# Loading x of batch 1 in front of the states, with every step of a hand-ordered attention and PReLU kernel placed anew

## The chip, the cores and the metric

The kernel runs on one core of one Trainium2 chip. The metric is the device time of one execution in microseconds, lower is better. The profiler takes one further execution of the same program; its span runs from the first to the last instruction, and its own time is given beside the median of the timed runs.

## The reference, cut to what matters

x is (8 batches, 8 heads, 512 tokens, 64), state is (8, 8, 32, 64), the model width 512 = 8 heads x 64, the hidden width 2048. Everything is float32 outside.

```python
def _attn_ref(x, state):
    scores = scale * np.matmul(x, state.transpose(0, 1, 3, 2))     # tokens read the states
    a = softmax(scores)
    xread = np.matmul(a, state)
    scores2 = scale * np.matmul(state, x.transpose(0, 1, 3, 2))    # states read the tokens
    a2 = softmax(scores2)
    sread = np.matmul(a2, x)
    return np.concatenate([xread, sread], axis=2)

def _moe_ref(x, w_in, w_out, alpha):
    h = x @ w_in
    g = np.maximum(h, 0.0) + alpha * np.minimum(h, 0.0)
    return g @ w_out
```

The output of the attention, 8 x (512 + 32) rows of 512, is the input of the second function.

## The kernel before

**What is computed where.** The token half of the attention never forms `xread`: state times w_in is made once per batch (`m`, four pieces f of 512 hidden columns, from quarter f of w_in), and the hidden layer of a batch is softmax weights times `m` (`F`, one of 16 pieces of 128 hidden rows by 512 tokens, two matmuls of 512 columns). `N` on ACT makes the negative part, `G` on DVE the PReLU result g. For batch 0 the output product is direct (`S`, sums over hidden pieces into one bank per 128 tokens, then `O` out); batches 1 to 7, and the state rows of all batches taken as batch 8, use a seven-product scheme of Strassen's kind (`P`, four matmuls of 256 columns each, into the banks px, py and pv). Its sums of weights are `W` and its sums of g are `U`, both on POOL; `K` saves an intermediate px, `Q` makes a quarter of the output and sends it with one or two DMAs on SP's queue.

**The softmax of a batch.** x of batch b is loaded as float16 by a casting DMA of 512 KB on POOL's queue (`lx.b`), transposed by a DMA on SP's queue (`xd.b`; for batches 0 and 1 by PE, `xt`, with copies `xo`), and multiplied with the states (`sc.b`). From `sc` two chains start: for the tokens' weights `sb`, `smax`, `ssh`, `sexp`, `ssum`, `snorm`, `wb` and then the first `F` of the batch; for the states' own reading `tm`, `nb`, `te`, `tsum`, `tn`, `tt` (a DMA transpose), `rd`. Batch 0 uses its own path (`tsc`, `smax`, `ssh`, `sexp`, `ssum`, `snorm`, then `at` on PE and the copies `ao`).

**The opening.** Half of x of batch 0 comes by two plain DMAs on SP's and ACT's queues (`dx`, then the casts `cx`), the other half by a casting DMA on POOL's queue (`dxp.1`, 256 KB). The states of batch 0 come on SP's queue (`dst`; `stc` casts, `stt` transposes, `sto` and `sbd` copy), those of batches 1 to 7 in two casting DMAs of 112 KB on POOL's queue (`lst.0`, `lst.1`; `str` transposes a half of them on PE, `sro` copies it). The quarters of w_in (`wi`) and w_out (`wo`), 512 KB each, follow on POOL's queue. `Z.k.n` are filler matmuls of n x 128 columns on a constant tile, in bank k, that compute nothing which is used.

**What sets the order.** The whole program is one string of steps, `ORDER` (lines 19 to 99). A loop at the end of the kernel (the dictionary `steps`) calls one small function for each token, in that order, so each engine's queue holds its instructions in the order of the string. The numbers and letters of a token are its arguments: batch and piece, the PSUM bank (the last number of `F`, `f`, `xt`, `str`, `rd` and of the first `P` of a bank; the last two of some `m`), and the engine (`a` ACT, `v` DVE, `p` POOL, `s` SP). Six banks, 0 to 5, are given out by these numbers; two more form one tile named `two`, which `sc` and the `m` without bank numbers use in turn. A bank can be written again only when the last reader of its former content is done.

**Lines.** `lx` is L162, `dxp` L172, `dx` L182, `lst` L223, `wi` L232, `wo` L238, `Z` L261, `str` L274, `xt` L325, `xo` L330, `sc` L340, `at` L391, `snorm` L439, `rd` L509, `m` L536, `mo` L560 and L562, `F` L589, `f` (a half of two `F` of batch 0) L611, `N` L642, `G` L645, `S` L659, `W` L703, `U` L727, `P` L748, `K` L764, `Q` L779 to L787.

```python
    for token in (globals().get("TOKENS") or ORDER).split():
        name, *args = token.split(".")
        steps[name](*[int(a) if a.isdigit() else a for a in args])
```

Of the kernel before, what the change touches and what calls it, by code (L numbers as in the profile page):

```python
# [29 lines left out]
tsum.1 S.0.0.0 sc.0.0 sc.0.1 m.0.3.1.3 mo.0.3.a.1 mo.0.3.a.0 tm.0 S.0.1.1.4 S.0.1.0 nb.0.a S.0.1.2 F.0.14.1 te.0.1  # L30
S.0.1.3 ssum.1.3 snorm.v.1 tn.1.1.p tn.1.0.p N.0.14 F.0.15.0 S.0.0.4 S.0.1.4 te.0.0 m.1.3 N.0.15 mo.1.3.a S.0.1.5
tsum.0 F.0.12.3 W.2.0.p tn.0.1.p N.0.12 G.0.15 tn.0.0.p S.0.3.4 F.0.13.0 G.0.14 N.0.13 wb.1 G.0.12 tt.0 m.1.2 S.0.1.7
F.1.7.1 N.1.7 xd.2 W.3.0.p F.1.2.3 N.1.2 G.0.13 S.0.0.6 G.1.7 W.2.1.p F.1.6.0 S.0.1.6 G.1.2 F.1.12.1 N.1.6 O.0.1.v
tt.1 S.0.0.5 F.1.3.3 G.1.6 F.1.5.4 S.0.0.7 W.4.1.p mo.1.2.a F.1.15.0 S.0.3.5 N.1.12 G.1.12 F.1.14.1 N.1.3 N.1.5 N.1.15
G.1.3 O.0.0.a W.3.1.p N.1.14 S.0.3.6 S.0.3.7 W.4.0.p G.1.5 G.1.15 G.1.14 m.2.2.3.4 sc.2 mo.2.2.a.0 rd.0.0 mo.2.2.a.1
F.1.1.1 F.1.4.4 rdo.0.a O.0.3.a F.1.8.0 sb.2 N.1.1 S.0.2.2.5 tm.2 smax.2 N.1.8 lx.3 F.1.13.2 N.1.4 G.1.4 nb.2.a
S.0.2.7 S.0.2.0 ssh.p.2 S.0.2.6 S.0.2.4 te.2.1 F.1.0.4 rd.1.3 G.1.1 te.2.0 G.1.8 N.1.13 m.3.2 m.2.3.0.1 N.1.0 tsum.2
G.1.13 rdo.1.v sexp.2 S.0.2.1 S.0.2.5 S.0.2.3 G.1.0 mo.2.3.a.1 F.1.11.4 mo.3.2.a F.1.9.1 P.1.1.1.1.3 P.1.1.0.0
mo.2.3.a.0 ssum.2.2 lx.4 O.0.2.a N.1.11 F.1.10.0 N.1.10 U.1.1.1.p snorm.v.2 P.1.1.1.0 str.1.5 wb.2 m.2.1 N.1.9 sro.1.a
P.1.1.0.1 F.2.15.2 G.1.11 N.2.15 G.1.10 P.1.2.1.1.4 tn.2.0.p P.1.2.0.1 G.1.9 mo.2.1.a F.2.1.5 F.2.14.1 N.2.1 P.1.2.0.0  # L40
m.3.1 G.2.15 m.3.0.0.2 xd.3 K.1.1.v G.2.1 P.1.2.1.0 U.1.3.1.p F.2.0.5 N.2.14 mo.3.0.a.0 mo.3.0.v.1 F.2.11.0 tn.2.1.p
mo.3.1.a G.2.14 tt.2 N.2.0 U.1.2.1.p U.1.1.0.p Q.1.0.0 F.2.2.2 N.2.11 P.1.6.0.1 G.2.0 U.1.2.0.p m.5.0 N.2.2 U.1.3.0.p
G.2.11 U.1.4.1.p rd.2.4 P.1.6.1.1 m.4.0.1.5 rdo.2.v mo.5.0.a m.3.3.4.0 sc.3 G.2.2 P.1.6.1.0 sb.3 mo.4.0.a.0 mo.3.3.a.0
mo.3.3.a.1 tm.3 F.2.7.1 F.2.5.2 P.1.7.1.1.4 P.1.6.0.0 mo.4.0.a.1 N.2.7 F.2.4.0 F.2.13.5 G.2.7 N.2.5 P.1.7.0.1 K.1.2.a
nb.3.a P.1.5.0.0 G.2.5 N.2.4 N.2.13 U.1.4.0.p P.1.5.1.0 smax.3 F.2.9.2 P.1.7.0.0 te.3.1 lx.5 F.2.8.1 G.2.13 te.3.0
P.1.5.0.1 G.2.4 N.2.9 N.2.8 G.2.9 F.2.3.5 tsum.3 P.1.5.1.1 xd.4 ssh.p.3 N.2.3 F.2.10.0 K.1.4.a F.2.12.2 G.2.8 N.2.10
P.1.7.1.0 G.2.3 N.2.12 F.2.6.1 P.1.3.1.1 G.2.10 G.2.12 m.6.0 sexp.3 m.4.1.0.5 P.1.3.1.0 P.1.3.0.1 N.2.6 Q.1.1.1
mo.4.1.a.1 mo.6.0.a mo.4.1.a.0 tn.3.0.p G.2.6 tn.3.1.p ssum.3.2 P.1.3.0.0 U.2.1.0.p P.1.4.0.1 m.6.1.1.5 m.4.3
mo.6.1.a.0 P.1.4.1.1 P.1.4.1.0 P.1.4.0.0 mo.6.1.a.1 P.2.1.1.1.1 snorm.v.3 P.2.1.1.0 mo.4.3.a Q.1.0.1.v wb.3 m.4.2.2.5
m.5.3.0.3 sc.4 mo.4.2.a.1 P.2.1.0.0 mo.5.3.a.1 U.2.1.1.p F.3.15.5 mo.4.2.a.0 Q.1.1.0 P.2.1.0.1 U.2.2.1.p F.3.4.3  # L50
mo.5.3.a.0 F.3.12.4 F.3.1.2 K.2.1.a F.3.8.0 N.3.15 sb.4 tm.4 U.2.2.0.p N.3.12 N.3.4 P.2.6.0.1 N.3.1 nb.4.a G.3.15
G.3.12 P.2.6.0.0 N.3.8 F.3.6.5 N.3.6 P.2.6.1.0 xd.5 G.3.4 G.3.1 G.3.6 P.2.6.1.1 G.3.8 U.2.3.0.p F.3.3.4 F.3.7.3
K.2.2.a te.4.1 N.3.3 F.3.14.2 smax.4 U.2.4.1.p P.2.5.1.0 N.3.14 tt.3 U.2.4.0.p G.3.14 F.3.2.0 N.3.2 ssh.p.4 P.2.5.1.1
P.2.5.0.0 te.4.0 F.3.11.5 P.2.5.0.1 G.3.3 N.3.7 G.3.2 F.3.0.2 rd.3.4 K.2.4.a sc.5 P.2.3.1.0 N.3.0 U.2.3.1.p P.2.3.0.1
G.3.7 N.3.11 G.3.0 rdo.3.a F.3.10.3 tm.5 P.2.7.1.0.0 tsum.4 P.2.3.1.1 G.3.11 P.2.3.0.0 N.3.10 tn.4.0.p nb.5.a F.3.9.4
sexp.4 P.2.7.0.0 P.2.7.0.1 Q.2.0.1.a G.3.10 P.2.7.1.1 P.2.2.0.0.2 lx.6 ssum.4.3 N.3.9 P.2.2.1.0 G.3.9 P.2.2.1.1
F.3.13.1 te.5.1 te.5.0 U.3.1.0.p Q.2.1.1 tn.4.1.a P.2.2.0.1 tsum.5 P.2.4.0.0 N.3.13 snorm.v.4 P.2.4.1.1 F.3.5.4
P.2.4.1.0 P.2.4.0.1 Q.2.0.0 wb.4 P.3.1.0.0.3 F.4.5.5 N.3.5 U.3.2.0.p tt.4 P.3.1.1.0 tn.5.0.a N.4.5 tn.5.1.p G.3.5
F.4.3.2 F.4.8.4 G.3.13 N.4.3 U.3.1.1.p Q.2.1.0 N.4.8 F.4.2.1 P.3.1.1.1 N.4.2 G.4.5 F.4.7.0 P.3.1.0.1 U.3.2.1.p G.4.3
F.4.14.2 U.3.3.1.p N.4.7 K.3.1.a G.4.8 tt.5 F.4.9.5 N.4.14 U.3.4.0.p G.4.2 G.4.7 F.4.10.4 U.3.3.0.p F.4.12.1 P.3.6.0.0  # L60
N.4.9 U.3.4.1.p G.4.14 P.3.6.1.0 F.4.11.0 N.4.12 P.3.6.0.1 G.4.9 N.4.10 F.4.6.5 P.3.6.1.1 sb.5 rd.4.2 lx.7 N.4.11
G.4.11 N.4.6 K.3.2.a G.4.12 xd.6 G.4.10 rdo.4.a rd.5.0 m.6.3 m.7.0.2.1 F.4.13.4 P.3.5.1.1 rdo.5.a P.3.5.0.0 mo.6.3.a
G.4.6 N.4.13 mo.7.0.v.0 F.4.15.2 m.7.3.5.0 sc.6 mo.7.0.a.1 smax.5 F.4.4.1 P.3.5.0.1 G.4.13 P.3.5.1.0 mo.7.3.a.0
P.3.7.1.1.5 N.4.15 mo.7.3.a.1 F.4.0.4 N.4.4 F.4.1.0 P.3.7.0.0 K.3.4.a P.3.7.0.1 sb.6 G.4.15 N.4.0 P.3.2.0.0.2 tm.6
P.3.7.1.0 P.3.3.1.1 P.3.3.0.0 smax.6 P.3.2.1.0 N.4.1 G.4.1 P.3.2.0.1 nb.6.a ssh.p.5 Q.3.1.1 te.6.0 P.3.2.1.1 P.3.4.0.0
G.4.0 P.3.4.1.1 sexp.5 te.6.1 G.4.4 Q.3.0.0 ssh.p.6 ssum.5.4 P.3.4.1.0 sexp.6 snorm.v.5 P.3.3.0.1 P.4.2.0.1.1 m.5.2
U.4.1.1.p m.6.2.0.2 U.4.1.0.p wb.5 P.3.4.0.1 P.4.2.1.1 mo.6.2.a.0 P.3.3.1.0 mo.6.2.a.1 mo.5.2.a xd.7 Q.3.0.1.a
U.4.2.1.p P.4.1.1.0.0 P.4.1.0.1 P.4.1.1.1 m.7.2.2.4 m.5.1 Q.3.1.0 mo.7.2.a.0 F.5.12.3 P.4.2.1.0 ssum.6.5 P.4.1.0.0
tsum.6 mo.7.2.a.1 mo.5.1.a K.4.1.a F.5.0.2 snorm.v.6 N.5.12 P.4.2.0.0 F.5.2.4 Q.4.0.0 U.4.2.0.p P.4.6.1.1 F.5.15.5
F.5.8.1 sc.7 P.4.6.0.1 P.4.6.1.0 G.5.12 N.5.2 P.4.6.0.0 G.5.2 tn.6.0.p N.5.0 G.5.0 N.5.15 U.4.3.0.p F.5.9.4 N.5.8  # L70
K.4.2.a G.5.15 F.5.1.3 N.5.1 F.5.5.2 G.5.8 tm.7 F.5.3.1 F.5.10.5 G.5.1 P.4.5.0.0 P.4.5.0.1 N.5.5 N.5.3 N.5.9 N.5.10
nb.7.a G.5.5 G.5.3 F.5.11.3 P.4.5.1.1 G.5.10 tn.6.1.p N.5.11 te.7.1 P.4.5.1.0 U.4.4.0.p F.5.6.2 K.4.4.a G.5.9
U.4.3.1.p U.4.4.1.p G.5.11 F.5.14.5 F.5.4.1 F.5.7.4 N.5.6 P.4.7.1.0.3 sb.7 P.4.7.1.1 P.4.3.1.0 P.4.3.0.0 N.5.14 N.5.7
P.4.7.0.1 P.4.7.0.0 G.5.6 P.4.3.1.1 F.5.13.2 P.4.3.0.1 te.7.0 G.5.7 G.5.14 N.5.13 U.5.1.0.p tt.6 wb.6 tsum.7 F.6.13.5
# [764 lines left out]
```

## Time and profile before

| what | value |
|---|---|
| median of 3 runs | 209.1 us (208.94 to 209.68) |
| the profiled execution's own time | 210.77 us |
| its span | 208.6 us |
| granted TensorE clock, mean | 0.997 |
| busy: PE | 202.1 us (97%) |
| busy: DVE | 174.8 us (84%) |
| busy: POOL | 181.5 us (87%) |
| busy: ACT | 146.1 us (70%) |

The profile's page gives busy time by engine, slices of the span, the chain of work that ended last, and groups of equal instructions. PE's share needs care: a matmul's end is modelled and overlaps the start of the next, so the distance from one start to the next is the true price. A row of the timeline gives the start, the length and the number of merged instructions; the bracket at its end is the idle time of the engine just before, and what ended it.

### The profile page before, as it was taken

Reading aid. Unit: us, or ns where it says so; the run is one execution under the profiler, and the core shown is the slowest. Engines: PE = TensorE matmul, PEld = TensorE weight load, DVE = VectorE, ACT = ScalarE, POOL = GpSimd, SP = SyncE. Lnnn points to the kernel's source line nnn. Section 1 sums busy time; section 2 is a strip of 40 time slices with the busy share of each in tenths; the row PEclk is TensorE's granted clock in tenths of the full one; section 3 lists DMA queues with packets and bytes.
Section 4 is the critical chain, followed back from the end, with each engine's and each line's share of the span. In section 5 each row is a group of like instructions: output and inputs, shape, how many; then the busy total and the mean of one; then the engine's idle time right before and its main releaser. Section 6 shows DMA issues by size and latency. Waiting matters only on the chain.

```text
span 208.6 us, 5096 instructions
## 1 busy us (share of the span) xinstructions
PE 202.1 (97%) x2012; PEld 135.2 (65%) x2012; DVE 174.8 (84%) x265; ACT 146.1 (70%) x286; POOL 181.5 (87%) x117
## 2 busy tenths in 40 slices
...
GB/s 141 180 206 207 207 204 90 220 124 120 165 172 102 86 70 203 52 5 231 206 67 24 182 175 97 34 50 152 53 0 53 75 25 3 50 50 104 50 125 128
DMA packets 44455, 23.43 MB, mean 112 GB/s; under 512 B 23696, under 2 KB 43920, under 8 KB 44432
## 3 DMA queue, kind: packets, MB, share of 16 engines
...
q8 instruction: 15, 0.25, 0.5%
...
HBM read 17.31 MB, written 8.91 MB: 126 GB/s over the span
## 4 chain that ended last, share of the span: by engine, by line
PE 87%; DMA 6%; POOL 4%; issue 1%; DVE 0%; POOLq 0%
PE h L589 25%; PE px L748 24%; PE pv L748 13%; PE o L659 6%; PE py L748 5%; DMA xg<-in_x_dram 4%; PE m_ps L536 4%; PE h L598 3%; POOL gsum L727 3%; PE sr_ps L509 2%; PE fill L261 2%; DMA e2T<-e 2%; PE sc L340 1%; POOL e L490 1%; PE h L611 1%
## 5 line engine op out<-in xcount | busy, mean ns | idle before, releaser
L645 DVE SCALAR_TENSOR_TENSOR g<-neg,oma_sb,h 128x512 f16<-128x512 f32 (+1 forms) x142 | 94.3, 709 | 11.0 <-ACT neg L642 9.9
L642 ACT ACTIVATE neg<-h 128x512 f32<-128x512 f32 (+1 forms) x142 | 75.6, 588 | 24.2 <-PE h L589 14.2
L589 PE MATMUL h<-aT,m 128*128 128x512 f16 x252 | 67.5, 379 | 0.0
L748 PEld LDWEIGHTS <-gsum 128*128 128x128 f16 x480 | 46.5, 98 | 14.5 <-issue 0.8
L748 PEld LDWEIGHTS <-g 128*128 128x128 f16 x360 | 34.8, 98 | 9.9 <-issue 1.7
L727 POOL TENSOR_TENSOR gsum<-g,g 128x1024 f16<-128x1024 f16 (+1 forms) x16 | 31.9, 2003 | 7.1 <-DVE g L645 7.0
L589 PEld LDWEIGHTS <-m 128*128 128x128 f16 x252 | 24.1, 98 | 17.2 <-issue 1.2
L727 POOL TENSOR_TENSOR gsum<-gsum,g 128x1024 f16<-128x1024 f16 (+1 forms) x16 | 32.0, 2008 | 0.7
L748 PE MATMUL px<-ws,gsum 128*128 128x256 f16 x240 | 32.5, 273 | 0.0
L727 POOL TENSOR_TENSOR gsum<-g 128x1024 f16<-128x1024 f16 (+1 forms) x16 | 32.0, 2007 | 0.0
L727 POOL TENSOR_TENSOR gsum<-g,gsum 128x1024 f16<-128x1024 f16 (+1 forms) x16 | 31.9, 2011 | 0.1
L764 ACT COPY kept<-px 128x512 f32<-128x512 f32 (+1 forms) x20 | 11.5, 573 | 15.8 <-PE px L748 15.7
L562 ACT CAST m<-m_ps 128x512 f16<-128x512 f32 x32 | 17.8, 601 | 5.9 <-PE m_ps L536 5.9
L410 POOL TENSOR_TENSOR ts<-ts,mx 128x1024 f32<-128x1024 f32 x7 | 13.4, 1919 | 5.6 <-DVE mx L405 5.6
L781 DVE TENSOR_TENSOR oq<-pv,kept 128x512 f32<-128x512 f32 (+1 forms) x16 | 10.4, 648 | 7.6 <-PE pv L748 4.2
L748 PE MATMUL px<-w_out_sb,g 128*128 128x256 f16 x120 | 16.7, 273 | 0.0
L748 PE MATMUL py<-w_out_sb,g 128*128 128x256 f16 x120 | 16.7, 273 | 0.0
L659 PE MATMUL o<-w_out_sb,g 128*128 128x512 f16 x64 | 16.6, 379 | 0.0
L748 PE MATMUL px<-w_out_sb,gsum 128*128 128x256 f16 x120 | 16.4, 273 | 0.0
L748 PE MATMUL pv<-ws,gsum 128*128 128x256 f16 x120 | 16.4, 273 | 0.0
L748 PE MATMUL pv<-ws,g 128*128 128x256 f16 x120 | 15.7, 273 | 0.0
L560 ACT CAST m<-m_ps 128x1024 f16<-128x1024 f32 x14 | 14.5, 1033 | 0.2 <-PE m_ps L536 0.2
...
## 6 DMA issues: line engine op xcount, KB each, us to landing
...
```

What stands on the lines that cost most here:

```text
L410: engine(e).tensor_tensor(blocks(cols(live["ts", b], j, S)), blocks(scored(b, j)), over_blocks(cols(live["mx", b], j, S // N)), ALU.subtract,)
L536: nc.tensor.matmul(t[N * k : N * (k + 1), :], st_head(b, h)[64 * r : 64 * r + 64, :], w_in_sb[64 * r : 64 * r + 64, c, 512 * f : 512 * (f ...
L560: copier(e)(m_tile(b, f), t)
L562: copier(e)(m_tile(b, f)[:, g, :], t[g])
L589: nc.tensor.matmul(h_g, ms[b, f][:, g, 128 * j : 128 * (j + 1)], weights(b, g), start=(g == 0), stop=(g == 1),)
L642: nc.scalar.activation(neg, h, RELU, bias=0.0, scale=-1.0)
L645: nc.vector.scalar_tensor_tensor(g_tile(b, jc), negs.pop((b, jc)), oma_sb[:, jc : jc + 1], hs.pop((b, jc)), ALU.mult, ALU.add,)
L659: nc.tensor.matmul(outs[b, q], g_tile(b, jc)[:, 128 * q : 128 * (q + 1)], w_out_sb[:, jc, :], start=not begun and jc == 2 * jc2, stop=left ...
L727: engine(e).tensor_tensor(t, x(), y(), op)
L748: nc.tensor.matmul(pbanks[b, name][:, i, :], of(b, c)[:, j, 128 * i : 128 * (i + 1)], moving[:, 4 * c + j, :], start=not begun and j == 0, ...
L764: copier(e)(t, pbanks[b, "x"])
L781: nc.vector.tensor_tensor(osb, pbanks[b, name], kept[b, add], ALU.add)
```

## The change

Only the string `ORDER` is changed; all functions stay as they are. Its 1113 tokens are the same steps, but for some engines and for the fills. The load of x of batch 1 (`lx.1`) moves in front of the load of the first half of the states (`lst.0`). All other steps are placed anew, and so are the banks. The fills are eight in both, 146 units of 128 columns before and 166 after. Some 30 steps change engine: of the opening `cx.0.1`, `xo.0.0.0`, `stc`, `sto`, one `sbd`, three of the four `xo.1` and `snorm.0.1`; later some `K`, `Q`, `mo`, `rdo` and `tn`.

The first lines of the string, and its last ones:

```diff
 ORDER = """
-dxp.1 mz io dx.0.0.4.s dx.0.4.8.a dst.s cx.0.0.v stc.a lst.0 id Z.0.29 Z.0.10 xt.0.0.0.5 cx.0.1.v stt.2 xt.0.0.1.1
-xo.0.0.0.v sto.a la sbd.0.v Z.0.10 sbd.1.v xo.0.0.1.v tsc.0.0.3 xt.0.1.1.4 xo.0.1.1.a tsc.0.1 xt.0.1.0.5 Z.0.7 str.0.1
-lx.1 tsc.1.1.2 wi.0 xo.0.1.0.a sro.0.a smax.0.0 tsc.1.0 ssh.v.0.0 smax.0.1 Z.0.29 wi.1 ssh.v.0.1 wi.2 sexp.0.0
-ssum.0.0 xt.1.0.0.3 xt.1.0.1.1 xt.1.1.0.4 sexp.0.1 ssum.0.1 xt.1.1.1.2 snorm.p.0.0 Z.0.24 wo.0 xo.1.0.1.a wo.1
-xo.1.1.0.a wi.3 wo.2 at.0.4 xo.1.1.1.a xo.1.0.0.a wo.3 snorm.v.0.1 m.0.0.2.5 m.1.0.1.3 oma.a mo.0.0.a.1 ao.0.v
-mo.1.0.a.0 mo.0.0.v.0 mo.1.0.a.1 at.1.4 ao.1.v sc.1 tm.1 f.0.0.0.2 n.0.0.0 m.2.0.4.1 f.0.0.1.3 mo.2.0.a.0 nb.1.a sb.1
-g.0.0.0.0 n.0.0.1 mo.2.0.a.1 Z.0.18 m.0.1.5.4 Z.0.19 g.0.0.1.1 mo.0.1.v.1 g.0.0.1.0 te.1.1 F.0.2.1 F.0.3.0 mo.0.1.a.0
+io dxp.1 dx.0.0.4.s mz dx.0.4.8.a cx.0.1.a Z.5.38 lx.1 cx.0.0.v id xt.0.0.0.3 Z.5.5 dst.s stc.v stt.4 lst.0 xo.0.0.0.a
+sto.v xt.0.0.1.1 la wi.0 Z.5.15 sbd.0.v sbd.1.a xo.0.0.1.v xt.0.1.0.0 tsc.0.0.2 tsc.0.1 wi.1 xt.0.1.1.3 Z.5.15
+smax.0.0 xo.0.1.0.a xo.0.1.1.a tsc.1.0.1 ssh.v.0.0 tsc.1.1 Z.5.42 sexp.0.0 wi.2 smax.0.1 xt.1.1.1.4 ssh.v.0.1 wo.0
+sexp.0.1 ssum.0.0 str.0.1 xt.1.0.1.2 ssum.0.1 wo.1 sro.0.a xo.1.1.1.v snorm.p.0.0 snorm.p.0.1 xt.1.1.0.3 xo.1.0.1.v
+xo.1.1.0.v wi.3 xt.1.0.0.0 Z.5.9 wo.2 lx.2 at.0.4 xo.1.0.0.a m.0.0.2.1 sc.1 m.1.0.0.3 oma.a mo.0.0.a.0 wo.3 W.1.0.p
+mo.1.0.a.1 ao.0.v mo.0.0.v.1 at.1.4 m.2.0.2.1 tm.1 mo.1.0.a.0 ao.1.v mo.2.0.a.0 nb.1.a Z.5.15 f.0.0.0.0 mo.2.0.a.1
+lst.1 n.0.0.0 F.0.3.3 F.0.2.2 sb.1 m.0.1.4.1 g.0.0.0.1 N.0.3 N.0.2 mo.0.1.a.1 g.0.0.0.0 Z.5.27 te.1.0 G.0.3 mo.0.1.v.0
...
-P.7.4.0.1 U.8.1.1.p Q.7.0.0 P.7.3.1.1 U.8.2.0.p K.8.1.v P.7.4.1.1 U.8.2.1.p P.7.4.1.0 P.7.4.0.0 P.8.6.0.1 P.8.6.0.0
-Q.7.1.0 U.8.3.1.p P.7.3.0.1 Q.7.0.1.v U.8.3.0.p K.8.2.a P.8.7.0.1.0 P.8.5.0.1 U.8.4.0.p P.8.5.0.0 K.8.4.a P.8.7.0.0
-U.8.4.1.p P.8.2.0.1 P.8.3.0.0 P.8.3.0.1 Q.8.1.1 P.8.4.0.0 P.8.4.0.1 Q.8.0.0 Q.8.0.1.v Q.8.1.0
+U.8.1.1.p U.8.3.0.p P.7.4.0.0 P.8.1.0.1 U.8.2.1.p Q.7.0.0 P.7.3.0.0 U.8.3.1.p Q.7.0.1.v K.8.1.a P.7.4.1.0 P.7.4.1.1
+P.8.6.0.0 P.8.6.0.1 Q.6.0.1.a P.8.2.0.1.3 P.8.7.0.0.4 Q.7.1.0 K.8.2.v P.8.5.0.0 P.8.5.0.1 U.8.4.1.p P.8.2.0.0 K.8.4.v
+P.8.7.0.1 P.8.3.0.1 Q.8.0.0 U.8.4.0.p Q.8.1.1 P.8.3.0.0 Q.8.0.1.v P.8.4.0.0 P.8.4.0.1 Q.8.1.0
 """
```

Three places show what moves. The first is POOL's queue in the opening, where all casting loads are issued. Before (`x2` and `x3` are equal instructions in a row):

```order
L172 DMA xg_69<-in_x_dram 128x8x128
L223 DMA st<-in_state_dram 128x448
masks.py:197 MEMSET ident 128x128
L162 DMA xg_177<-in_x_dram 128x8x256
L232 DMA w_in_sb<-in_moe_w_in_dram 128x4x512 x3
L439 TENSOR_TENSOR an_190<-ts_187,r_0_189 128x512
L238 DMA w_out_sb<-in_moe_w_out_dram 128x4x512 x2
L232 DMA w_in_sb<-in_moe_w_in_dram 128x4x512
L238 DMA w_out_sb<-in_moe_w_out_dram 128x4x512 x2
L410 TENSOR_TENSOR ts_338<-ts_338,mx_339 128x1024
L162 DMA xg_414<-in_x_dram 128x8x256
L703 TENSOR_TENSOR ws_421<-w_out_sb 128x1024 x2
```

Now:

```order
L172 DMA xg_69<-in_x_dram 128x8x128
L162 DMA xg_101<-in_x_dram 128x8x256
masks.py:197 MEMSET ident 128x128
L223 DMA st<-in_state_dram 128x448
L232 DMA w_in_sb<-in_moe_w_in_dram 128x4x512 x3
L238 DMA w_out_sb<-in_moe_w_out_dram 128x4x512 x2
L439 TENSOR_TENSOR an_172<-ts_169,r_0_171 128x512 x2
L232 DMA w_in_sb<-in_moe_w_in_dram 128x4x512
L238 DMA w_out_sb<-in_moe_w_out_dram 128x4x512
L162 DMA xg_256<-in_x_dram 128x8x256
L238 DMA w_out_sb<-in_moe_w_out_dram 128x4x512
L703 TENSOR_TENSOR ws_306<-w_out_sb 128x1024
```

The 512 KB of x of batch 1 now stand ahead of the 112 KB of states, the first quarter of w_in stays behind both; two quarters of w_out pass the softmax product of batch 0, which now has both its halves on POOL, x of batch 2 passes the last quarter of w_out, and the first sum of weights passes `ssh.p.1` (L410).

The second place is ACT in the opening, from the copies of batch 0's transposes to the first casts of `m`. Before:

```order
L330 COPY xT_126<-xT_ps_1_0_155 128x4x128
L308 COPY stT<-st_ps_162 128x896
L419 ACTIVATE ts_187<-ts_187 128x512 x2
L330 COPY xT_244<-xT_ps_0_1_218 128x4x128
L330 COPY xT_244<-xT_ps_1_0_223 128x4x128
L330 COPY xT_244<-xT_ps_1_1_231 128x4x128
L330 COPY xT_244<-xT_ps_0_0_213 128x4x128
L299 ACTIVATE oma_sb<-alpha_sb 128x16
L562 CAST m_0_281<-m_ps_0_1_260 128x512
```

Now:

```order
L330 COPY xT_124<-xT_ps_1_1_160 128x4x128
L419 ACTIVATE ts_169<-ts_169 128x512 x2
L308 COPY stT<-st_ps_211 128x896
L330 COPY xT_235<-xT_ps_0_0_247 128x4x128
L299 ACTIVATE oma_sb<-alpha_sb 128x16
L562 CAST m_0_303<-m_ps_0_0_264 128x512
```

The copy of the transposed states (L308, `sro.0`) moves behind the two exponentials, and three of the four copies of batch 1's transposes leave ACT for DVE.

The third place is ACT in batch 2, around the second `K` of that batch (L764, `K.2.2`), which saves px before a product adds to it. Before:

```order
L462 ACTIVATE nb_1487<-nb_1487 128x2
L642 ACTIVATE neg_8_1509<-h_8_1477 128x512
L642 ACTIVATE neg_6_1514<-h_6_1511 128x512
L764 COPY kept_2_1541<-px_1387 128x512
L472 ACTIVATE e_4_1543,r_4_1544<-sc_1424,nb_1487 128x512
```

Now:

```order
L642 ACTIVATE neg_8_1535<-h_8_1492 128x512
L462 ACTIVATE nb_1480<-nb_1480 128x2
L642 ACTIVATE neg_4_1544<-h_4_1515 128x512
L472 ACTIVATE e_4_1547,r_4_1548<-sc_1428,nb_1480 128x512
L764 COPY kept_2_1550<-px_1402 128x512
```

The exponential of batch 4 (L472) now stands directly ahead of that copy, where it stood behind it.

More of the change, by code (lines that the diff above doesn't have):

```diff
@@ L30 @@
[L30 to L74, printed above, removed]
```

93 lines of the change are left out of this document (69 added, 24 removed).

## The prediction, made before the result was known

> **What bounds the kernel now.** I read the windows of busy time first, split at 14.90 us, where the first product with w_in starts, then PE's list of waits, then the timeline around that split and around the end.
>
> ```profile
> core 0: us, PE busy (x), PEclk, DMA share, GB/s
> 0.00:14.90 14.90, 12.21 (x101) 1.00 1.09 174
> 14.90:204.90 190.00, 189.84 (x1913) 1.00 0.55 107
> ```
>
> From 14.90 us to its last matmul PE is busy for 189.84 of 190.00 us, at the full granted clock (1.00). A modelled end can hide a short pause, so PE's waits after the opening are the cross-check (tile, what it waited for, us in total, times, longest):
>
> ```profile
> PE xT_ps L325 <- DMA xg<-in_x_dram: 1.1, 1, 1.1
> PE sr_ps L509 <- DMA e2T<-e: 0.2, 1, 0.2
> ```
>
> After the wait for x of batch 1 (it ends at 12.33) there is one of 0.2 us in the whole run. So the span has three parts: 14.90 us until w_in is there, 190.0 us of matmuls without a gap, and 3.7 us behind them. What starts that clock at 14.90 is a transfer:
>
> ```profile
> 1.25 1.09 POOL L172 DMA_DIRECT2D xg<-in_x_dram  x1 [0.80 <-POOLq L823]
> 2.34 0.56 POOL L223 DMA_DIRECT2D st<-in_state_dram  x1
> 3.43 0.92 POOL L162 DMA_DIRECT2D xg<-in_x_dram  x1
> 4.35 2.32 POOL L232 DMA_DIRECT2D w_in_sb<-in_moe_w_in_dram  x3
> 12.12 1.05 POOL L439 TENSOR_TENSOR an<-ts,r 128x512 f16<-128x512 f32 x1 [5.45 <-DVE r L429]
> ...
> 3.43 8.85 DMA xg<-in_x_dram
> ...
> 14.90 0.29 PEld L536 LDWEIGHTS <-stT 64*32 64x32 f16 x16 [0.16 <-DMA w_in_sb<-in_moe_w_in_dram]
> ...
> DMA  0000000134589999999999999999999999999999
> ```
>
> The last row is the first 10 us in 40 slices: the DMA engines are 90% busy from 3.0 us on. POOL's queue issued its loads within 7 us, and they land one after the other: x of batch 1 at 3.43 + 8.85 = 12.28, the first quarter of w_in at about 14.85 (it ended PE's wait). The landing of the states comes from the group of the tile st in that window, whose longest of two is this load, and gives 2.34 + 5.8 = 8.1:
>
> ```profile
> DMA to landing us min/median/max: 4.0/4.9/5.8
> ```
>
> **The change, part by part.** *The load that moves.* The same 256 + 112 + 512 KB stand ahead of the first quarter of w_in, in another order, in a queue that is never empty, so w_in lands at 14.85 as before: 0. What changes is inside: x of batch 1 should land where the states no longer push it back, about 112 KB earlier. The nearest price is 2.57 us for 512 KB (14.85 - 12.28), so 0.6 us earlier at 11.7; the states land last, at 12.3. I bound w_in's landing by 0.5 us on either side (about those 112 KB at that price).
>
> The Trainium skill, "DMA: Bandwidth & Descriptors", section "Queues, rings and completion order", says that each of the 16 engines takes its ring's descriptors in order, but that a load counts as landed only when all its engines have reported, so completion is not first in, first out per issuer. By that rule the states, spread over the slowest ring too, are complete only behind that ring's share of x. The trace agrees in the old order, where x, issued behind the states, landed 4.2 us after them; by the rule and by the rows alike the sum gets 0 from w_in, but the rule speaks against putting a small, needed load behind a large one, and the second rival below prices that.
>
> *PE until w_in.* Now `xt.1.1.1`, then `str.0.1` (states), three more `xt`, a fill of 9 units and `at.0` stand in PE's queue ahead of `m.0.0`.
>
> ```profile
> 8.71 0.58 PE L274 MATMUL st_ps<-ident,st 128*64 128x128 f16 x14
> ...
> 12.33 1.07 PE L325 MATMUL xT_ps<-ident,xg 128*128 128x128 f16 x16 [1.14 <-DMA xg<-in_x_dram]
> 13.23 1.46 PE L261 MATMUL fill<-pattern 128*128 128x512 f16 x6
> 14.53 0.39 PE L391 MATMUL at_ps<-ident,an 128*128 128x128 f16 x4
> ...
> 79.32 1.73 PE h L589 x8
> ```
>
> From start to start 16 `xt` matmuls take 0.90 (12.33 to 13.23), `str` 0.51 (8.71 to the next at 9.22), `at` 0.37 (14.53 to 14.90), and a matmul of 512 columns 0.216 (1.73 / 8), so a fill unit of 128 columns 0.054. From the states at 12.3: 0.51 + 0.68 + 0.49 + 0.37 = 2.05, so PE stands at `m.0.0` at 14.35 and waits 0.5 us for w_in. That is the cover: states up to 0.5 us late cost nothing. The softmax of batch 0 is inside it: `at.0` needs the POOL product that ends at 12.12 + 1.05 = 13.17; its second half, now also on POOL, ends at 14.22, and `at.1` is due at 15.6. Two more weight loads issued ahead of it cost POOL 2 x 0.77 us (2.32 / 3) out of the 5.45 us in which it sat idle before that product.
>
> *PE after w_in.* All products are the same, so three differences count.
>
> ```profile
> 15.35 0.69 DVE L562 CAST m<-m_ps 128x512 f16<-128x512 f32 x1
> ...
> 14.90 0.63 PE L536 MATMUL m_ps<-w_in_sb,stT 64*32 64x512 f16 x16
> 15.46 0.40 PE L391 MATMUL at_ps<-ident,an 128*128 128x128 f16 x4
> 15.79 0.41 PE L340 MATMUL sc<-xT,stT 64*32 64x256 f16 x16
> 16.13 0.61 PE L611 MATMUL h<-aT,m 128*128 128x256 f16 x4
> ...
> 28.77 0.42 PE L340 MATMUL sc<-xT,stT 64*32 64x128 f16 x32
> 29.02 0.44 PE L536 MATMUL m_ps<-w_in_sb,stT 64*32 64x512 f16 x8
> ```
>
> Fills behind `m.0.0`: 18 + 19 = 37 units before, 15 + 27 = 42 now: 5 x 0.054 = +0.27. `sc.1`: alone between full-size matmuls it took 0.34 (15.79 to 16.13); inside a stretch of small-tile steps 32 such matmuls took 0.25, so 16 take 0.13: now it stands inside one, -0.21. From there on such stretches are as many as before (25 in each program from `m.0.0` on), so I take 0 for the rest, within 0.3. `m.2.0` now needs the banks of `m.0.0`: 14.90 + 0.56 (two `m`, 14.90 to 15.46) + 0.13 + 0.37 puts PE there at 15.96, while the DVE cast that frees one ends at 15.35 + 0.69 = 16.04, and I add 0.1 for the signal: +0.18.
>
> I followed the first 14 us behind that by the same rows; ACT and DVE are then the engines that PE leans on, and three covers are thin. The first is behind these rows of DVE:
>
> ```profile
> 15.96 0.41 DVE L394 COPY aT<-at_ps 128x512 f16<-128x512 f16 x1
> 16.29 1.21 DVE L455 TENSOR_REDUCE nb<-sc 128x2 f32<-128x1024 f32 x1
> 17.42 1.24 DVE L372 STREAM_TRANSPOSE ts<-sc 128x1024 f32<-128x1024 f32 x1
> ```
>
> `F.0.3` wants the second copy of the weights, behind `tm.1` on DVE: 16.04 + 1.13 (16.29 to 17.42) + 0.41 = 17.6, PE is there at 17.7. The cast on DVE that `F.0.7` wants and `te.1.1` on ACT that `m.0.2` wants come out 0.1 and 0.5 us ahead of PE. If these covers are gone, I price it at 0.1 to 0.3 us each.
>
> *POOL and SP behind the opening.* `W.1.0` waits for the first quarter of w_out (14.85 + 3 x 2.57 = 22.6) and now holds `lst.1` and `ssh.p.1`, which ends near 27.1; its user on ACT stands behind steps that end near 27.6. x of batch 2 passes a quarter of w_out and lands one 512 KB piece, 2.6 us, earlier. Counted through at 2.1 us for a sum, each `U` of batches 1 to 4 is done at least 1.7 us before its product (before: 0.7). All 0.
>
> *The end.* One more output quarter, `Q.6.0.1`, now stands among the last, so SP issues two more DMAs there.
>
> ```profile
> 195.86 7.12 SPq L785 DMA_DIRECT2D out_dram<-oq  x8
> 203.33 2.67 SPq L787 DMA_DIRECT2D out_dram<-oq  x4
> ...
> 203.93 1.04 PE L748 MATMUL pv<-ws,g 128*128 128x256 f16 x8
> ...
> 205.01 0.42 DVE L781 TENSOR_TENSOR oq<-pv,kept 128x256 f32<-128x256 f32 x1 [0.45 <-PE pv L748]
> ```
>
> At about 0.6 us an issue (2.67 / 4 at most) SP is through with them near 202.7, and the buffer that the last quarter reuses is free near 204.1, before DVE wants it at 205.0. 0; if that cover of 0.9 us is gone, up to +0.5.
>
> **Sum.** +0.27 - 0.21 + 0.18 = +0.24 on a span of 208.6, so about 208.8. The median of the runs (209.1) lies 0.5 above that span, while the profiled execution's own time is 210.77; I hold span to median: 209.1 + 0.2 = 209.3.
>
> **The rivals.** *Late reads of banks (slower).* px is saved by `K` or `Q` before the next product adds to it, and PE stands if the read is late. The shortest distance that held before:
>
> ```profile
> 172.52 1.04 PE L748 MATMUL px<-ws,gsum 128*128 128x256 f16 x8
> 173.40 0.60 PE L598 MATMUL h<-XS,w_in_sb 128*128 128x256 f16 x4
> 173.83 0.59 PE L589 MATMUL h<-aT,m 128*128 128x512 f16 x2
> 174.26 0.27 PE L748 MATMUL px<-ws,gsum 128*128 128x256 f16 x1
> ...
> 173.60 0.59 ACT L764 COPY kept<-px 128x512 f32<-128x512 f32 x1 [0.66 <-PE px L748]
> ```
>
> The last write gives way at 173.40, the read ends at 174.19, and the next write starts at 174.26: 0.86 us just do, with ACT idle beforehand. By the same prices from start to start three reads stood at this distance before and the next at 1.3; now seven stand at it and two more under 1.1, two of the nine where ACT is nearly full (`K.2.2` right behind an exponential, and `Q.1.0.1`). For it speaks that nothing is left if ACT is late; against it, that by the rows ACT reaches `K.2.2` at 82.8 and px is complete at 82.9. Each late read costs up to one ACT step, 0.6; from two full ones on it is 1.2 us: 210.5.
>
> *The states come late (slower).* If they land with w_in, at 14.85, `str.0.1` holds PE, and the 2.05 us counted above follow: 14.85 + 2.05 = 16.9 instead of 14.9, +2.0: 211.3. It decides from 12.8 on. For it speaks the place behind 512 KB; against it, that the queue's bytes ahead are those that were through at 12.28. The Trainium skill, "TensorE: Matmul & The Clock Gate" (table at its head), says that PE pulls only weight loads ahead, matmuls stay in order; by that rule nothing behind `str.0.1` could fill the wait.
>
> *w_in lands earlier (faster).* If the new order serves 0.5 us of bytes sooner, PE at 14.35 can use all of it; with the extra fill that is 208.8, still no change that could be told. For a larger gain the states and the softmax would have to be sooner too; nothing in the rows shows that. With 1.3 us: 208.0.
>
> **How the numbers follow.** A measurement here tells about 0.5% (1.05 us) from no change. Forecast 209.3, its own range 208.4 to 210.1: 0.58. Late reads, 210.5: 0.2, of which a fifth stays within 0.5%. Late states, 211.3: 0.08. Faster by over 0.5%, near 208.0: 0.14. So faster 0.14, same 0.58 + 0.04 = 0.62, slower 0.16 + 0.08 = 0.24. The range takes in the bounds of w_in's landing and of the stretches below (208.3) and the late reads above (210.9).
>
> **What would show it.** Right: `m.0.0` starts at 14.9 with a wait for w_in before it; PE busy for all but 0.5 us from there on; 3.7 us behind the last matmul. The states' landing before 12.8 settles the second rival; waits of PE's P matmuls on ACT's or DVE's reads of px would show the first. It is wrong if `m.0.0` starts over 0.7 us away from 14.9, or PE's pauses behind it add up to over a microsecond.

## The result, and the profile after

| what | before | changed |
|---|---|---|
| median of 20 runs each | 209.43 us (208.69 to 211.08) | 210.82 us (210.05 to 211.46) |
| ratio of the times | | 1.0054, 95% interval 1.0034 to 1.0074 |
| the profiled execution's own time | 210.77 us | 210.96 us |
| its span | 208.6 us | 209.2 us |

The changed kernel is slower by 1.1 to 1.4 us (by the ratio, by the medians), a little over half a per cent. The two profiled spans differ by only 0.6 us, because the execution shown of before was a late one: its own time is 1.3 us over its median. Timed beside the experiments, before has a median span of 207.5 us (96 runs, median time 209.4 us); the changed kernel has one of 209.05 us (20 runs). So 1.55 us of span have to be found.

The windows of busy time of the changed kernel, split where `m.0.0` starts and where PE is done (window, length, PE busy and its instructions, granted clock, DMA share, GB/s):

```profile
0.00:13.65 13.65, 12.46 (x104) 1.00 1.09 170
13.65:204.05 190.40, 190.16 (x1913) 1.00 0.55 108
204.05:209.20 5.15, 0.06 (x1) 0.77 0.27 92
```

PE starts on w_in's products at 13.65 instead of 14.90, is busy for nearly all of 190.4 us instead of 190.0, and is done some 0.85 us earlier than in the execution before. Behind it come 5.15 us instead of 3.7. In these two profiles the loss is at the end, not in the opening. PE's list of waits agrees; beside the wait at the start there is one, for w_out:

```profile
PE fill L261 <- DVE pattern L215: 1.1, 1, 1.1
PE o L659 <- DMA w_out_sb<-in_moe_w_out_dram: 0.2, 1, 0.2
```

The timeline of the last microseconds of the changed kernel, from its queue of output DMAs (SPq) to the last quarter on DVE, and the last step of the chain of waits:

```profile
195.75 6.76 SPq L785 DMA_DIRECT2D out_dram<-oq  x10
202.61 3.94 SPq L787 DMA_DIRECT2D out_dram<-oq  x4
...
203.07 1.04 PE L748 MATMUL pv<-ws,g 128*128 128x256 f16 x8
203.33 0.42 DVE L779 COPY oq<-px 128x256 f32<-128x256 f32 x1 [0.50 <-PE px L748]
205.56 0.42 DVE L781 TENSOR_TENSOR oq<-pv,kept 128x256 f32<-128x256 f32 x1 [1.80 <-DMA out_dram<-oq]
...
201.93 3.55 DMA out_dram<-oq
```

In the kernel before, the last quarter on DVE waited 0.45 us for PE. Here it waits 1.80 us for an output DMA: the one issued at 201.93, the second of `Q.7.1.0`, whose buffer the last quarter takes over, lands 3.55 us after its issue, where the median of these DMAs is 2.2 us. And four issues on SP take 3.94 us instead of 2.67. The same is seen in the DMA engines. The window of 204.5 to 205.3 us, first of the kernel before:

```profile
DMA packets 176, 0.16 MB, mean 205 GB/s; under 512 B 16, under 2 KB 176, under 8 KB 176
out_dram<-oq SPq DMA_DIRECT2D x2, 128.0 KB, 2.1
```

and of the changed kernel:

```profile
DMA packets 15, 0.01 MB, mean 18 GB/s; under 512 B 1, under 2 KB 15, under 8 KB 15
out_dram<-oq SPq DMA_DIRECT2D x2, 128.0 KB, 2.5
```

For nearly a microsecond single packets trickle through. The trace has 16 landing signals for each output DMA, as many as there are DMA engines, and they say where it hangs: of the DMA issued at 201.93, 14 came by 204.13, one at 204.58 and the last at 205.48. One part was late by 1.3 us, and the landing waited for it. What stands ahead of that gap is in the queues of the window of 202.5 to 206.5 us of the changed kernel:

```profile
q1 hardware_dynamic: 720, 0.66, 49.3%
q8 instruction: 1, 0.02, 2.0%
q14 instruction: 1, 0.01, 0.6%
```

Queue q8 loads instructions. One packet of 16 KB took 2.0% of 16 engines' 4 us, which is 1.28 us on one engine; it starts at 203.0. That is as long as the last signal above was late. The page has 16 such packets in the span (0.26 MB), one for about each 252 of the 4034 matmuls and weight loads in PE's record, which points to PE's program as what they load (e7 below bears it out: 158 more of them move the load 8 us forward). In the kernel before, with 4024, the page has 15 in the span, and the sixteenth starts at 209.6, when the span of 208.6 is over. The window of 209.5 to 209.7 us of before:

```profile
q8 instruction: 1, 0.02, 43.9%
```

The 8 KB on q14 are no difference between the two: in every profile such a load starts between 202.6 and 204.6 us, in the kernel before at 204.3.

The Trainium skill, "Runtime: NRT & Kernel Launch", section "Instruction fetch mechanics", says that an engine's instructions are refilled in blocks of 16 KiB, 256 instructions, over a DMA queue of its own, and that crossing a block is mostly hidden. The sizes agree with this trace, and for PE it was hidden (busy for 190.16 of 190.40 us); whether it was hidden from the other DMAs was for the experiments to say.

### The profile page after: what moved, and what is told of

Read it like the earlier page. It is cut to its first block, busy times and chain, and to the rows that moved or that the text cites. A ratio compares the mean times of both kernels' runs of the same rounds, so it can differ in the third digit from the quotient of the medians.

```text
span 209.2 us, 5110 instructions
## 1 busy us (share of the span) xinstructions
PE 202.7 (97%) x2017; PEld 135.6 (65%) x2017; DVE 174.6 (83%) x267; ACT 146.7 (70%) x286; POOL 180.6 (86%) x115
## 4 chain that ended last, share of the span: by engine, by line
PE 84%; DMA 9%; POOL 2%; SPq 1%; issue 1%; DVE 1%; DVEq 0%; POOLq 0%
PE h L589 25%; PE px L748 24%; PE pv L748 11%; DMA w_out_sb<-in_moe_w_out_dram 7%; PE o L659 7%; PE py L748 6%; PE m_ps L536 4%; PE h L598 3%; PE sr_ps L509 2%; DMA out_dram<-oq 2%; SPq L785 1%; POOL w_in_sb L232 1%; PE sc L340 1%; POOL xg L162 0%; DVE oq L779 0%
## 5 line engine op out<-in xcount | busy, mean ns | idle before, releaser
L589 PE MATMUL h<-aT,m 128*128 128x512 f16 x252 | 66.7, 379 | 0.0
L748 PEld LDWEIGHTS <-gsum 128*128 128x128 f16 x480 | 46.4, 98 | 13.1 <-issue 1.0
L748 PEld LDWEIGHTS <-g 128*128 128x128 f16 x360 | 34.5, 98 | 10.9 <-issue 2.4
L748 PE MATMUL px<-ws,gsum 128*128 128x256 f16 x240 | 31.6, 273 | 0.0
L748 PE MATMUL py<-w_out_sb,g 128*128 128x256 f16 x120 | 17.7, 273 | 0.0
L764 ACT COPY kept<-px 128x512 f32<-128x512 f32 (+1 forms) x18 | 10.4, 579 | 10.0 <-PE px L748 9.7
L748 PE MATMUL px<-w_out_sb,g 128*128 128x256 f16 x120 | 16.6, 273 | 0.0
L748 PE MATMUL pv<-ws,gsum 128*128 128x256 f16 x120 | 16.2, 273 | 0.0
L748 PE MATMUL pv<-ws,g 128*128 128x256 f16 x120 | 16.1, 273 | 0.0
L748 PE MATMUL px<-w_out_sb,gsum 128*128 128x256 f16 x120 | 16.0, 273 | 0.0
L410 POOL TENSOR_TENSOR ts<-ts,mx 128x1024 f32<-128x1024 f32 x7 | 13.4, 1913 | 1.2 <-DVE mx L405 1.2
```

The source lines that it names most:

```text
L410: engine(e).tensor_tensor(blocks(cols(live["ts", b], j, S)), blocks(scored(b, j)), over_blocks(cols(live["mx", b], j, S // N)), ALU.subtract,)
L589: nc.tensor.matmul(h_g, ms[b, f][:, g, 128 * j : 128 * (j + 1)], weights(b, g), start=(g == 0), stop=(g == 1),)
L748: nc.tensor.matmul(pbanks[b, name][:, i, :], of(b, c)[:, j, 128 * i : 128 * (i + 1)], moving[:, 4 * c + j, :], start=not begun and j == 0, ...
L764: copier(e)(t, pbanks[b, "x"])
```

## The experiments

The theory that these rows suggest: the loss is at the end, because `Q.6.0.1` now stands among the last quarters. Its rivals: the loss is in the loads or in PE's pauses, or the 1.80 us were a chance of one execution. Each run lists the kernel's median and its ratio to the kernel before, timed beside it (209.25 to 209.51 us). The tail below is the time from the start of the last eight products (a row like `203.07 1.04 PE L748` above) to the end of the span; it is 4.67 us before and 6.13 us changed.

**Q.6.0.1 early (e1).**

```diff
-K.7.1.a P.7.6.1.1 ... P.8.6.0.1 Q.6.0.1.a
+K.7.1.a Q.6.0.1.a P.7.6.1.1 ... P.8.6.0.1
```

> The changed kernel with Q.6.0.1 put back to an early place (right behind K.7.1), all else as changed. Theory (the end: the two output DMAs of Q.6.0.1 among the last ones push the second DMA of Q.7.1.0 to 201.9 us, whose landing at 205.5 the last quarter waits for): that DMA is issued about 1.2 us earlier, the 1.8 us wait of DVE before the last quarter falls to about 0.5 us for PE, the stretch behind the last matmul falls from 5.3 to about 4.3 us, and the time by 0.9 us, from 210.8 to about 209.9. Rival (that wait was one late landing in one profiled execution, and the loss lies in PE's pauses or in the loads): the time stays within 0.3 us of 210.8.

211.30 us, 1.0083 (1.0056 to 1.0109): a miss, though the wait for the buffer was gone (0.45 us, for PE). The place was badly chosen: on ACT the copy of 0.59 us now stood ahead of two `N`, and PE's waits got a new row; and SP still lost a microsecond in its four last issues.

```profile
PE h L597 <- DVE g L644: 1.0, 1, 1.0
...
203.39 3.62 SPq L786 DMA_DIRECT2D out_dram<-oq  x4
```

The tail was 5.55 us. So something holds up the end besides the place of `Q.6.0.1`; an instruction load falls among the output DMAs here too (it starts at 204.1), and the issue on SP behind it takes 1.70 us.

**Buffers of their own (e2).**

```diff
-tag="osb", bufs=4
+tag="osb" if b < B else "neg", bufs=4
```

> The changed kernel, order untouched, but the four quarters of batch 8 take buffers that are idle by then (those of the tiles neg), so no quarter waits for an output DMA's landing. Theory (the end): SP issues as late as before, but the last quarter follows PE at once, near 204.6 instead of 205.56 us, and the time falls by 0.9 us to about 209.9. If the queue of SP itself were the limit and not the buffer, the last DMA would still be issued near 206.0 and the time would fall by less than 0.3 us. Rival (loss elsewhere): no change, 210.8 within 0.3.

209.91 us, 1.0022 (1.0006 to 1.0038), as the theory had it. The tail is 5.31 us: DVE follows PE at once, and SP's issues stay slow (3.17 us for four).

**Q.6.0.1 late in the kernel before (e3).**

```diff
-F.8.10.2 Q.6.0.1.v P.7.6.0.0 F.8.5.3
+F.8.10.2 P.7.6.0.0 F.8.5.0
-F.8.14.3
+F.8.14.2
-P.8.6.0.0 Q.7.1.0
+P.8.6.0.0 Q.6.0.1.v Q.7.1.0
```

> The kernel before with Q.6.0.1 moved right in front of Q.7.1.0 (and two pieces F of batch 8 in other banks, since px of batch 6 holds its bank longer). Theory (the end): SP issues two more DMAs from 199.5 on, the last DMA of Q.7.0.1 moves from 202.4 to between 202.9 and 203.6 and lands near 205.3 to 206, so the last quarter waits 0.3 to 0.8 us and the time rises by as much, from 209.4 to between 209.7 and 210.2. Rival (loss elsewhere): 209.4 within 0.3.

210.47 us, 1.0053 (1.0031 to 1.0074): the theory's sign, and a little more than its price. The tail is 5.12 us, 0.45 more than before, without any load on q8 in it; the last quarter waits for a buffer:

```profile
195.81 7.50 SPq L784 DMA_DIRECT2D out_dram<-oq  x10
203.41 3.00 SPq L786 DMA_DIRECT2D out_dram<-oq  x4
...
205.41 0.42 DVE L780 TENSOR_TENSOR oq<-pv,kept 128x256 f32<-128x256 f32 x1 [0.91 <-DMA out_dram<-oq]
```

From `m.0.0` to the last eight products it took 189.2 us, 0.2 more than before; the rest of the 1.07 us lies within the interval.

**The swap of the loads alone (e4).**

```diff
-stc.a lst.0 id
+stc.a lx.1 lst.0 id
-str.0.1 lx.1 tsc.1.1.2 wi.0 xo.0.1.0.a sro.0.a
+tsc.1.1.2 wi.0 xo.0.1.0.a
-xt.1.1.1.2
+xt.1.1.1.2 str.0.5
-xo.1.0.1.a
+sro.0.a xo.1.0.1.a
```

> The kernel before with only the swap of the loads: x of batch 1 in front of the states on POOL's queue, and the transpose of the states (str, sro) behind the first transpose of x of batch 1, since they land later now. Theory (the swap is worth nothing by itself): w_in's first quarter lands within 0.5 us of 14.85, m.0.0 starts near 14.9, time 209.4 within 0.4. Rival (the swap itself brings w_in 1.2 us earlier, as the changed kernel's trace has it): m.0.0 can start no sooner than the softmax of batch 0 lets at.0 run, near 13.9 to 14.5, so 0.4 to 1.0 us faster, 208.4 to 209.0. Second rival (the swap delays PE): str waits for the states at 12.3 and pushes x's transposes and the fills, up to 0.5 us slower.

210.47 us, 1.0056 (1.0037 to 1.0075). All three expectations missed. w_in landed early (8.8 us after its issue, at 13.1), but PE reached `m.0.0` at 14.47 only, behind a wait of `at.0` for a copy of a transpose on ACT:

```profile
PE at_ps L390 <- ACT xT L329: 0.6, 1, 0.6
```

And the tail is 6.06 us: here the instruction load starts at 206.3, and the last output DMA, issued at 205.1, lands at 208.5 instead of 2.1 us later: 15 of its 16 signals came by 207.1. So a load alone, with `Q.6.0.1` early, cost 1.4 us of tail in this execution (it was a late one, 211.32 us, 0.85 over the median). PE has as many matmuls and weight loads here as before (4024); with that count the load stands at an edge: behind the span in before, nowhere in the record of e3, and inside the span here.

**Where the load falls (e5, e6, e7).** Fills are the one thing that changes PE's count without changing its work: shorter ones (e5), or the same columns in more matmuls (e6, e7). A third number in a token is the width of a piece:

```diff
 e5, changed kernel
-Z.5.38 Z.5.42
+Z.5.18 Z.5.14
 e6, kernel before
-Z.0.24
+Z.0.24.2
 e7, changed kernel
-Z.5.42 Z.5.38 Z.5.27
+Z.5.42.1 Z.5.38.1 Z.5.27.1
```

> The changed kernel with two fills of the opening shortened (Z.5.38 to 18 units, Z.5.42 to 14), so that PE's program has 24 instructions fewer; all real work as changed. Theory (a load of 16 KB of PE's instructions, which in the changed kernel runs from 203.0 to 204.3 us in the midst of the output DMAs, holds one DMA engine, delays the landing at 205.5 and SP's next issue by 1.4 us): it moves behind the last matmul, the span falls from 209.05 by about 1.0 us to 208.0; what lies outside the span may rise from 1.75 to 2.1, so 209.8 to 210.2 us. Rival (SP's backlog alone, the two more DMAs of Q.6.0.1): 210.8 within 0.3. If the shorter fills cost clock, the granted clock and the opening show it, and the time is above 211.

> The kernel before with one fill (Z.0.24) as 12 matmuls of 256 columns instead of 6 of 512: the same columns, PE's program 12 instructions longer. Theory (the instruction load): it moves from behind the span to about 203 us, among the output DMAs, and costs 0.8 to 1.3 us: 210.2 to 210.7, with less outside the span (1.75 instead of 1.9 to 2.7). Rival (the load of instructions is harmless): 209.4 within 0.3.

> The changed kernel with three fills (Z.5.42, Z.5.38, Z.5.27) cut into matmuls of 128 columns: the same columns, PE's program 158 instructions longer. Theory (the instruction load): it moves from 203.0 to about 194.5 us, in front of the run of output DMAs that begins at 195.75, nothing is delayed at the end, and the time falls by about 1.0 us to 209.6 to 210.0, with 1.75 outside the span. Rival (SP's backlog alone): 210.8 within 0.3.

The times: e5 211.32 us, 1.0076 (1.0052 to 1.0100); e6 209.51 us, 1.0005 (0.9988 to 1.0023); e7 211.51 us, 1.0082 (1.0050 to 1.0114). By the times all three expectations of the theory missed. The traces show why. The load went where it was sent: none before the end in e5, at 202.9 in e6, at 195.1 in e7. The tails followed: 5.12 and 5.22 us instead of 6.13 in e5 and e7, and 5.11 instead of 4.67 in e6, where SP's four last issues took longer than the 2.67 us of before, without any wait for a buffer:

```profile
q8 instruction: 1, 0.02, 1.9%
...
201.99 3.13 SPq L786 DMA_DIRECT2D out_dram<-oq  x4
...
203.66 0.42 DVE L780 TENSOR_TENSOR oq<-pv,kept 128x256 f32<-128x256 f32 x1 [0.45 <-PE pv L747]
```

(The first row is from the queues of 202.5 to 206.5 us.) But e5 and e7 lost time in front of the end: `m.0.0` started at 15.36 and 14.54, and in e7 PE later waited 0.8 us for a transposing DMA of the states' reading. In e5 the first fill ends at 3.2, PE stands until x is there at 4.96, and then runs at half its speed until about 10.9. First e5, then the changed kernel, where the fill lasts until x is there:

```profile
1.06 2.10 PE L260 MATMUL fill<-pattern 128*128 128x512 f16 x5 [1.06 <-DVE pattern L214]
4.96 0.61 PE L324 MATMUL xT_ps<-ident,xg 128*128 128x128 f16 x4 [1.80 <-DVE xg L187]
6.78 1.81 PE L260 MATMUL fill<-pattern 128*128 128x512 f16 x4
```

```profile
1.06 4.24 PE L261 MATMUL fill<-pattern 128*128 128x512 f16 x10 [1.06 <-DVE pattern L215]
6.33 0.97 PE L261 MATMUL fill<-pattern 128*128 128x512 f16 x4
```

The fill in the last row of each is the same `Z.5.15`, 15 units in four matmuls: 1.81 us in the one, 0.97 us in the other. So these two tell of the end by their tails alone, and e6's cost is too small for its interval: it is 0.44 us by the tail of one execution, while its timed runs lie 0.1 us above the kernel before in time and 0.2 us in span. By the times alone, a load moved in with the columns kept is not shown to cost anything.

**The loads put back (e8).**

```diff
-lx.1 cx.0.0.v id xt.0.0.0.3 Z.5.5 dst.s stc.v stt.4 lst.0
+lst.0 lx.1 cx.0.0.v id xt.0.0.0.3 Z.5.5 dst.s stc.v stt.4
```

> The changed kernel with the first half of the states in front of x of batch 1 again on POOL's queue, all else as changed. If the order of the loads is what brings w_in's first quarter earlier (13.1 to 13.7 us with x first in four traces, 14.6 to 14.9 with the states first in two): it lands at 14.6 to 14.9 again, PE starts m.0.0 about 1.0 us later and the time rises by 0.7 to 1.2 us, to 211.5 to 212.0. Rival (the landing is scatter between executions, or the bytes' place on the queue does not matter): 210.8 within 0.3.

210.88 us, 1.0064 (1.0045 to 1.0082), beside 210.82 changed: the rival. The order of these two loads is worth nothing that these runs can measure. w_in's first quarter lands at 4.3 plus the smallest of these numbers, in e8, in e6 and in the changed kernel:

```profile
DMA to landing us min/median/max: 9.2/12.6/13.3
```

```profile
DMA to landing us min/median/max: 8.2/10.7/12.6
```

```profile
DMA to landing us min/median/max: 9.3/12.8/13.8
```

That is 13.5, 12.6 and 13.6. Over all profiled executions it was 12.6 to 14.85 with the states first (5 of them), 13.1 to 13.9 with x first (9): scatter from one execution to the next, and the 14.85 of the profile before was its late end.

**The two causes taken away one by one (e9, e10, e11).** `Q.6.0.1` at a place where ACT is idle (e9), the fills cut to multiples of four units, 8 matmuls fewer (e11), both (e10):

```diff
 e9, e10
-N.8.8 ... P.8.6.0.1 Q.6.0.1.a
+N.8.8 Q.6.0.1.a ... P.8.6.0.1
 e10, e11
-Z.5.38 Z.5.5 Z.5.15 Z.5.15 Z.5.42 Z.5.9 Z.5.15 Z.5.27
+Z.5.36 Z.5.4 Z.5.12 Z.5.12 Z.5.40 Z.5.8 Z.5.12 Z.5.24
```

> The changed kernel with Q.6.0.1 moved to where ACT is idle (behind N.8.8, 189 us), all else as changed, the instruction load still at 203 us. Theory (two causes at the end, each near 0.45 us alone and 1.4 together: Q.6.0.1 among the last quarters, and the 16 KB load of PE's instructions among the output DMAs): PE loses nothing this time, the last quarter follows PE (idle near 0.5 us, not 1.8), SP's long issue stays, the stretch from the start of the last eight products to the end falls from 6.1 to about 5.1 us, time 209.8 (209.5 to 210.1). Rival (the loads and PE's pauses): 210.8 within 0.3.

> As the run before, and every fill cut to a multiple of four units (166 to 148 units, 8 matmuls and so 16 instructions of PE fewer), so that the instruction load comes behind the last matmul. Theory: the stretch from the start of the last eight products to the end is 4.7 us as in the kernel before, and the fills behind m.0.0 (6 units fewer) give up to 0.3 us: time 209.1 to 209.6, no longer slower than the kernel before by more than 0.2. Rival (PE's pauses and the opening make up the loss): above 210.

> The changed kernel with the shorter fills alone, Q.6.0.1 late as changed. Theory: no instruction load among the output DMAs, the last quarter still waits for a buffer, but only near 0.9 us; the stretch from the start of the last eight products to the end is 5.1 us, time 209.7 to 210.1. Rival (the load of instructions is harmless, only the place of Q.6.0.1 counts): 210.5 to 210.8.

e9: 209.99 us, 1.0036 (1.0015 to 1.0057). e11: 209.52 us, 1.0003 (0.9985 to 1.0022). e10: 208.86 us, 0.9984 (0.9965 to 1.0004). All three came out on the theory's side, e10 and e11 some 0.2 us under its ranges. The shorter fills take more than the load away: six of their units lie behind `m.0.0`, 0.3 us at 0.054 each, so the 1.1 us between the changed kernel and e11 are not the load's alone. The end of e10 reads like that of the kernel before:

```profile
199.94 0.59 SPq L784 DMA_DIRECT2D out_dram<-oq  x1
201.73 2.72 SPq L786 DMA_DIRECT2D out_dram<-oq  x4
...
202.38 1.04 PE L747 MATMUL pv<-ws,g 128*128 128x256 f16 x8
203.46 0.42 DVE L780 TENSOR_TENSOR oq<-pv,kept 128x256 f32<-128x256 f32 x1 [0.45 <-PE pv L747]
```

**The control (e12).** The kernel before with its fills cut alike, 5 units of them behind `m.0.0`:

```diff
-Z.0.29 Z.0.10 Z.0.10 Z.0.7 Z.0.29 Z.0.24 Z.0.18 Z.0.19
+Z.0.28 Z.0.8 Z.0.8 Z.0.4 Z.0.28 Z.0.24 Z.0.16 Z.0.16
```

> The kernel before with every fill cut to a multiple of four units (146 to 132, 7 matmuls fewer; 5 of the units lie behind m.0.0). It is the control of the run e10, which is 0.4 us under the kernel before. If e10's gain comes from its fills alone (0.054 us for each unit behind m.0.0), this one gains too: 0.27 us of PE and 0.1 us outside the span, where the load of PE's instructions now falls, so 209.0 us. If it comes from the new placing, this one stays at 209.3 within 0.15 while PE waits where the fills stood.

209.32 us, 0.9987 (0.9966 to 1.0009), beside 209.51 for the kernel before: by the time alone it lies between the two expectations. In its trace `m.0.0` to the last eight products takes 188.74 us instead of 189.03, about the 0.27 that the units behind `m.0.0` cost. But that does not explain e10: e10 has 36 units behind `m.0.0` and the kernel before 37, which is 0.05 us, not 0.4. The intervals of e10 and e12 both reach 1.0, so neither is told from the kernel before, and whether the new placing adds something stays open.

The tails side by side, each from one profiled execution:

| in the tail | runs | us |
|---|---|---|
| neither cause | before, e10, e12 | 4.67, 4.72, 4.68 |
| `Q.6.0.1` late alone | e3, e5, e7, e11 | 5.12, 5.12, 5.22, 5.34 |
| the instruction load alone | e6, e9, e1, e4 | 5.11, 5.29, 5.55, 6.06 |
| both | changed, e8 | 6.13, 6.01 |
| both, buffers of their own | e2 | 5.31 |

Over the 4.7 us without either, `Q.6.0.1` late costs 0.4 to 0.7 us, the load 0.4 to 1.4, depending on which DMA it meets (in e4 the very last one), and both together 1.3 to 1.5. That both together cost more than their sum is not shown: in the four kernels of the new placing the tails grow by 0.62 (e11), 0.57 (e9) and 1.41 (both), each in one execution, but the ratios of the timed runs add up, 0.9984 with neither (e10), plus 0.0019 (e11) and 0.0052 (e9), against plus 0.0070 with both. What the times do show is that with both taken away the loss is gone (1.0054 to 0.9984, 1.5 us), of which the shorter fills are some 0.3 us by the price of 0.054.

The spans add up too. Usual executions of before's order start `m.0.0` at 13.7 (e6, e12): 13.7 + 189.0 + 4.7 = 207.4, with a median span of 207.5. Changed: 13.6 + 189.0 to 189.4 + 6.1 = 208.7 to 209.1, with a median of 209.05. So the 1.55 us are 1.4 at the end and 0 to 0.4 in PE's stretch behind `m.0.0`; the opening is alike. Why the end has no slack is argued from the rows: ten DMAs stand back to back on SP, and in the changed kernel the load holds the one DMA whose buffer the last quarter needs.

## Why the prediction was right and wrong, point by point

**The number: inside by luck.** The forecast was +0.2 us, and +1.1 to 1.4 came, at 1.0054 a little past the 0.5% that it called a change; the slower side had a chance of 0.24. 210.82 us lies inside the stated bounds only because these were widened to 210.9 for late reads of banks, which did not happen; the main forecast ended at 210.1.

**The opening: the order right, the start wrong.** The order of the loads was forecast to be worth nothing to w_in; with the landing's scatter known, no order of the two loads shows an effect (e8). But `m.0.0` started at 13.65, 1.25 us from the forecast 14.9 and past the 0.7 us that the prediction named as its sign of being wrong: it took the landing of one late execution, 14.85, for the rule. The times inside it came from the same trace: x of batch 1 landed at 10.5 instead of 11.7, the states at 11.0 instead of 12.3, `at.0` ran at 13.13 instead of 13.98, and the cover at `m.0.0` was 0.15 us instead of 0.5 (13.13 + 0.37, against a start at 13.65).

**From span to median: off, but it cancelled, by luck.** The 0.5 us between span and median rested on a late execution. About 1.8 us lie outside the span, and before's usual span is 207.5. As before and changed shift alike, only the reading of the first profile suffered.

**Behind `m.0.0`: near in the sum, not in its terms.** +0.24 was forecast. From `m.0.0` to the last eight products it takes 189.42 us in the changed profile and 189.03 before; in e2 and e8, with the same stretch, 189.01. So it is 0 to +0.4, and 0.2 of the upper end is the wait for w_out in PE's list: a floor that the sum didn't have, since PE now comes to the first `S` before w_out has landed. `sc.1` takes 0.22 from its start to the next step (13.88 to 14.10), where the sum took 0.13; and `m.2.0` starts 1.10 us behind `m.0.0`, not the 1.24 of the sum, with no wait for a bank in PE's list. These two errors of about 0.1 us cancel. The price of 0.054 us for a fill unit is not settled by single traces: 5 fewer gave 0.29 in e12, 6 fewer only 0.14 in e10 (188.87 beside 189.01).

**The thin covers and POOL: right.** None of them appears among PE's waits.

**The end: wrong, and it is nearly the whole result.** By the prediction "the buffer that the last quarter reuses is free near 204.1, before DVE wants it at 205.0", priced at 0 and at most +0.5. It was free at 205.5, the tail grew by 1.4 us, and 5.15 us instead of 3.7 came behind the last matmul. Two things failed there. The cover of 0.9 us was worked out with each output DMA landing 2.1 us after its issue, as the others do, and `Q.6.0.1` alone did take about half a microsecond (e3), the upper bound. And the change's ten further instructions of PE (five fill matmuls with their weights) were priced by their columns only, +0.27 for the units behind `m.0.0` and 0 for those in the opening; with them the load of PE's code came at 203.0 instead of 209.6, as 12 more instructions did in the kernel before (e6: 202.9). The row of these loads (q8, 15 of them) stands on the page of before; when each falls could have been asked there.

**The rivals.** Late reads of banks: no wait of PE for a read of px in any profile of the changed kernel, so by these the distance of 0.86 us holds. States late: they landed at 11.0. w_in earlier: the changed profile looks like it (13.6), but it was scatter, not the order. The slower side came by a mechanism that none of them named.
